# Second forward stage of a spectral block as runs of 32 half-width products, with rows and chunks requested a run ahead

## The chip, the cores and the metric

The kernel runs on one core of a Trainium2 chip. The metric is the device time of one execution in microseconds; the times given are medians of several executions. Engines are called PE (matmul), DVE (vector), ACT (scalar), POOL (GpSimd) and SP, whose queue issues all the DMA transfers of this kernel. A loaded weight tile and a matmul are two instructions of PE; the weight loads are listed as PEld.

## What is computed

For 8 sequences of 3136 positions and 256 channels: a real Fourier transform along the sequence, a complex 256 by 256 product with bias and soft threshold for each frequency, the inverse transform, and on its result y a mixing block: the real part of a two-dimensional transform is added, rows are normalised, and an MLP with 1024 hidden units is added to them.

```python
X = np.fft.rfft(x, axis=1);  Yr = Xr @ w_r - Xi @ w_i + b_r;  Yi = Xr @ w_i + Xi @ w_r + b_i
Y = soft_threshold(Yr, 0.01) + 1j * soft_threshold(Yi, 0.01)
y = np.fft.irfft(Y, n=3136, axis=1)
u = y + real(fft(fft(y, axis=1), axis=2))
un = (u - mean(u)) / sqrt(var(u) + 1e-6)
out = u + relu(un @ w_ch1) @ w_ch2
```

## The kernel before

The sequence length is split as 64 x 49. Work on each sequence b (0 to 7) is written as ten generators: p1 (first forward stage: products over the 64), p2_f2 (second forward stage: products over the 49, for both parts), p2_w (the complex product), p2_mix and p2_yt (mixing transform and transposes), p2_g2 (inverse over the 49), p3_norm (inverse over the 64, sum and normalisation), p3_tr (transposes), p3_mlp1 and p3_mlp2. Each generator yields a time of its own plan (in units of T, one sequence), and a heap resumes the one with the earliest time; so these times set the program order. A planner then puts the instructions of each engine in a fixed order by that priority and by what it expects to be ready. On the chip every engine works off its list in that order and waits where an operand or a buffer is not there.

Accumulators lie in eight PSUM banks: two for the MLP's first product (tile h, name h), two for its second (o), and four, tag g, that all other stages share (names g_f1, g_f2, g_w, g_mix, g_yt, g_g2, g_g1, g_ut). The MLP and most of the later stages use mm3: three products of rounded high and low parts (fp32r). The forward products of p1 and p2_f2 are plain f32; such a product becomes two weight loads and two matmuls on PE.

p2_f2 (lines 499 to 550) treats a sequence in four quarters q of eight frequencies. For each q, rows_f2 (line 484) requests two tiles af of 98 rows by 1024 and two tables tff (each of four frequencies, s = 0, 1). Then for four units ui it takes a bank and makes four products (line 523): weights are 128 columns of af (k = 0, 1), the moving operand is 100 columns of the table. ACT copies the bank to xx (line 539) and casts it to Xh (540); POOL or DVE subtracts (Xl); DVE adds the two parts (xs), ACT casts to Xsh (549), POOL subtracts to Xsl. For ui = 3 Xh is cast from the bank (545), one part is copied (546), and DVE does addition and Xl from the bank (547, 548). From sequence 2 on the work of a quarter is planned over 0.395 of its step, 0.25 T.

quarters (line 397) is used by p1 from sequence 1 on and by p3_norm. It makes eight products of 64 rows by 64 columns by 512 in four banks, for the four quarters of the array, as one block: small copies on ACT (line 403) hold the other banks until the rows have come, the first product waits for them, and the rest follow it directly.

ask (line 387) requests the chunks of x for p1 (tile xf, two buffers); from sequence 2 on it is called where the chunk's products are written. p3_norm requests bf (four buffers) and mt (two) for one pair of row groups at a time (load, line 799, called at line 820), just before its products at 832.

Of the kernel before, what the change touches and what calls it, by code (L numbers as in the profile page):

```python
# [20 lines left out]
D = 256  # L21
# [3 lines left out]
NM = 25  # L25
# [115 lines left out]
T1, ASK, BEHIND = (1.32, 0.25), 1.16, 3  # L141
WTIMES = (1.002, 1.003, 1.151, 1.152, 1.36, 1.42, 1.48, 1.54)
MLAG, NRM, TR = 1.874, -1.239, -0.86


@with_exitstack
def spectral_block(ctx: ExitStack, tc: tile.TileContext, x, w_ri, b_ri, w1, w2,
# [13 lines left out]
    def gtile(name):  # L161
        return ps.tile([128, 512], F32, tag="g", bufs=4, name=name)
# [146 lines left out]
    def after(*keys):  # L309
        while not all(k in done for k in keys):  # L310
            yield now[0] + 10
# [104 lines left out]
    def p1(b):  # L416

        if b == 0:
            yield from p1_first()
            return  # L420
        for i in (b, b + 1)[:1 + (b % 2 == 0)]:
            if i not in a_dram:
                ad = dr.tile([NM, 2, 2, U, D], F32, tag="ad", bufs=4, name=f"ad{i}")
                a_dram[i] = lambda u, ad=ad: (ad, u)
        todo = [(m, 4) for m in range(0, NM - 1, 4)] + [(NM - 1, 1)] * (b % 2 == 0)
        t0, width = T1 if b == 1 else (b - 0.3, 0.75) if b > 2 else (2.0, 0.48)
        rooms = [("W2", 1, 2), ("W3", 1, 2)] + [("utl", 2, 1)] * 2 if b == 1 else [("xf", 2, 1)] * len(todo)
        slots = [(tag, bufs, z, i) for tag, bufs, z in rooms for i in range(z)]
        evs = [("bf", 4)] * 4 + [("ev", 2)] * 2 if b == 1 else [("ev", 2)]
        pre = {}  # L430
        if b == 1:
            yield T * ASK
            for ci in range(len(todo)):
                ask(b, ci, todo, slots, pre)
        ci = 0
        while ci < len(todo):
            yield T * (t0 + width * ci / len(todo))
            if todo[ci][1] == 1:
                ask(b, ci, todo, slots, pre)
                m, xf = todo[ci][0], pre[ci]  # L440
                g = gtile("g_f1")
                te.matmul(g[:, :D], fwd_f, xf[:, :D], start=True, stop=True)
                ev = xf[:, D:2 * D]
                sc.copy(ev, g[:, :D])
                for r in range(2):
                    st_eng.dma_start(out=a_dram[b + r](0)[0][m, 0].rearrange("c u d -> (c u) d"), in_=ev[r * 64:r * 64 + 64])
                ci += 1
                continue
            groups = []
            for c in range(ci, ci + (1 if b == 1 else 2)):  # L450
                ask(b, c, todo, slots, pre)
                i = slots[c][3]
                xf = pre[c - i][:, i * 1024:i * 1024 + 1024]
                groups.append(([gtile("g_f1") for _ in range(2)],
                               [[xf[64 * r:64 * r + 64, p * 512:p * 512 + 512] for p in range(2)] for r in range(2)], xf[0:1, 0:2]))
            quarters(fwd_f, groups)
            for c, (banks, movs, late) in enumerate(groups, ci):
                xf, m = pre[c - slots[c][3]], todo[c][0]
                for r, g in enumerate(banks):
                    if b == 1:  # L460
                        tag, bufs = evs[(2 * c + r) % len(evs)]
                        ev = sb.tile([128, 512], F32, tag=tag, bufs=bufs, name="ev")
                    else:
                        ev = xf[:, r * 512:r * 512 + 512]
                    (va.tensor_copy if r and b != 1 else sc.copy)(ev, g)
                    st_eng.dma_start(out=n2_rows(a_dram[b](0)[0], m + 2 * r, 2), in_=ev.rearrange("p (n d) -> p n d", d=D))
            ci += len(groups)
        done.add(("a", b))

    def clock2(b, q):  # L470
        f2w, w0, ww = SHAPE if b else SHAPE0
        step = T * ((STEP0, STEP1)[b] if b < 2 else STEP)
        t0 = T * (1.0, START1)[b] if b < 2 else T * (b + 2 - LEAD - LAST * (b == NB - 1))
        return t0 + step * q, step, f2w, w0, ww, w0 + ww
# [3 lines left out]
    def x_tiles():  # L478


        return [sb.tile([128, 2] + c + [8, S], F32R, tag=t + z, bufs=1, name=t + z)
                for t, c in (("X", [2]), ("Xs", [])) for z in "hl"]

    def rows_f2(b, q, s):
# [11 lines left out]
            done.add(("af", 2 * q + s))  # L496
        return af, tff

    def p2_f2(b):


        for q in range(4):
            base, STEP, F2W, W0, WW, M0 = clock2(b, q)
            u0 = 8 * q
            yield base
            yield from after(("a", b, q) if b == 0 else ("a", b))
            if b == 0:
                X = sb.tile([128, 2, 2, 8, S], F32, tag=("Xh", "Xl")[q % 2], bufs=1, name="X")
                Xs = sb.tile([128, 2, 8, S], F32, tag=("Xsh", "Xsl")[q % 2], bufs=1, name="Xs")
                xt[b, q] = X, Xs  # L510
            else:
                xt[b, q] = Xh, Xl, Xsh, Xsl = x_tiles()
            afs, tfs = zip(*[rows_f2(b, q, s) for s in range(2)])
            for ui in range(4):
                yield base + STEP * ui * F2W / 4
# [251 lines left out]
    def p3_norm(b):  # L767

        def add(m, n, g, mt):

            ut = uts[b, m] = sb.tile([128, 2, D], F32, tag="ut", bufs=UTB, name="ut")
            va.tensor_add(ut[:, :n], g[:, :n * D].rearrange("p (n d) -> p n d", d=D), mt)  # L772
# [39 lines left out]
                af_ld.setdefault("mt", nc.sync.dma_start(out=mt[p:p + 32, :n], in_=mpn[:, n2:n2 + n]).ins)  # L812
            return mt, bfs
        pairs = ([[0], [4]] if b == 0 else [[0, 4]]) + [[8, 12], [16, 20]]
        for ms in pairs + [[NM - 1]] * (b % 2):
            n = 1 if ms[0] == NM - 1 else 4
            t0, T3 = clock3(b, ms[0])
            yield t0 + T3 * (NRM - 0.5 * (n == 1))
            yield from after(("b", b), ("m", b))
            loads = [load(m, n) for m in ms]  # L820
            if n == 1:
                mt, bfs = loads[0]
                g = gtile("g_g1")
                te.matmul(g[:, :D], inv_f, bfs[0][:, :D], start=True, stop=True)
                add(ms[0], 1, g, mt[:, :1])
                finish(ms[0], 1)
                continue
            if b == 0 and ms[0] == 0:
                yield from after(("w", 1, 0))
            groups = [([gtile("g_g1") for _ in range(2)], [[bfs[r][64 * p:64 * p + 64] for r in range(2)] for p in range(2)], bfs[0][0:1, 0:2])  # L830
                      for mt, bfs in loads]
            quarters(inv_f, groups, w_in[1, 0] if b == 0 and ms[0] == 0 else None)
            parts = [(m + 2 * p, g, mt[:, 2 * p:2 * p + 2]) for m, (mt, bfs), (banks, movs, late) in zip(ms, loads, groups) for p, g in enumerate(banks)]
            for m, g, mt in parts:
                add(m, 2, g, mt)
            for m, g, mt in parts:
                finish(m, 2)

# [165 lines left out]
```

## Time and profile before

| | us |
|---|---|
| median of 3 runs (1840.67 to 1847.36) | 1842.6 |
| profiled execution | 1843.72 |
| its span, first to last instruction | 1841.9 |
| PE busy | 1803.2 |
| DVE, ACT, POOL busy | 1210.2, 808.3, 564.8 |

Times in the rows are microseconds from the start of the span unless marked ns. Busy time is the time in which at least one instruction of an engine ran. Matmuls are pipelined: a record lasts from its start until its last result is written, and the next one starts before that. The chain that ended last is followed back from the last instruction, at each step to what released it. A line such as L175 can be that of a helper (mm3), so the tile names tell the stage.

### The profile page before, as it was taken

What the parts mean: (1) busy time and instruction counts of PE and PEld (TensorE: products, weight loads), DVE (VectorE), ACT (ScalarE), POOL (GpSimd) and SP (SyncE); (2) the same over time, 40 slices, a digit from 0 to 9 for tenths busy, and PEclk for the clock granted to TensorE, in tenths of its full rate; (3) what the DMA queues carried; (4) which work ended last, traced back from release to release, by engine and by line L of the source; (5) the groups of instructions that cost most, each with busy time, mean ns of one, the idle gap of its engine ahead of it and who ended that gap; (6) DMA issues with size and microseconds to landing.
All of it is one profiled execution on the core that took longest, in us unless ns stands there. A gap on an engine that the chain in (4) does not pass through costs nothing.

```text
span 1841.9 us, 29443 instructions
## 1 busy us (share of the span) xinstructions
PE 1803.2 (98%) x10082; PEld 1500.9 (81%) x10082; DVE 1210.2 (66%) x2619; ACT 808.3 (44%) x1914; POOL 564.8 (31%) x1021
## 2 busy tenths in 40 slices
PE   8988899999999999999999999999999999999998
PEld 5667688888888988888888988888888898878888
DVE  3866767676577766765776766757657767755543
ACT  2564454544445534444544444444444454322222
POOL 0003434333234332342432333423324334221110
PEclk8999899999999999999999999999999999999999
DMA  8766553554436533374515734345533533152211
GB/s 255 233 208 168 147 189 100 161 153 145 130 82 198 163 120 106 100 206 125 175 46 141 217 122 134 99 132 163 152 99 90 177 90 104 57 151 67 60 35 34
DMA packets 157936, 245.61 MB, mean 133 GB/s; under 512 B 24209, under 2 KB 105177, under 8 KB 157529
## 3 DMA queue, kind: packets, MB, share of 16 engines
q1 hardware_dynamic: 157784, 243.72, 45.2%
q8 instruction: 80, 1.31, 0.3%
q14 instruction: 72, 0.58, 0.1%
HBM read 140.79 MB, written 102.86 MB: 132 GB/s over the span
## 4 chain that ended last, share of the span: by engine, by line
PE 87%; DVE 5%; DMA 3%; SPq 2%; ACT 1%; issue 1%; POOL 1%; DVEq 0%; ACTq 0%; POOLq 0%
PE o L175 28%; PE h L175 27%; PE g_w L175 9%; PE g_f L523 5%; PE g_g L175 4%; PE g_yt L723 3%; PE g_g L402 2%; PE g_ut L853 2%; PE g_f L402 2%; PE g_w L569 2%; PE g_mix L660 1%; PE g_mix L662 1%; DMA out_dram<-total 1%; DMA md<-mq 1%; DVE ut L772 1%
## 5 line engine op out<-in xcount | busy, mean ns | idle before, releaser
L872 DVE SCALAR_TENSOR_TENSOR hl<-h,hh 128x512 fp32r<-128x512 f32 (+2 forms) x416 | 271.6, 655 | 391.2 <-ACT hh L871 388.2
L871 ACT ACTIVATE hh<-h 128x512 fp32r<-128x512 f32 (+2 forms) x416 | 237.5, 572 | 503.8 <-PE h L175 463.1
L175 PE MATMUL o<-hl,w2h 128*128 128x512 f32 (+2 forms) x832 | 329.0, 396 | 2.8 <-DVE hl L872 2.6
L175 PE MATMUL h<-utl,w1h 128*128 128x512 f32 (+2 forms) x832 | 319.5, 384 | 3.9 <-DVE hl L872 3.9
L175 PE MATMUL o<-hh,w2l 128*128 128x512 f32 (+2 forms) x832 | 318.5, 383 | 0.0
L175 PE MATMUL o<-hh,w2h 128*128 128x512 f32 (+2 forms) x832 | 317.1, 381 | 0.0
L175 PE MATMUL h<-uth,w1l 128*128 128x512 f32 (+2 forms) x832 | 316.0, 380 | 0.0
L175 PE MATMUL h<-uth,w1h 128*128 128x512 f32 (+2 forms) x832 | 315.7, 379 | 0.0
L879 POOL TENSOR_TENSOR total<-uth,utl 128x256 f32<-128x256 f32 x200 | 149.4, 772 | 476.4 <-DMA out_dram<-total 263.5
L175 PEld LDWEIGHTS o<-hl,w2h 128*128 128x128 f32 x832 | 157.0, 189 | 47.6 <-DVE hl L872 20.7
L175 PEld LDWEIGHTS h<-utl,w1h 128*128 128x128 f32 x832 | 156.7, 188 | 34.9 <-DVE hl L872 6.9
L175 PEld LDWEIGHTS h<-uth,w1l 128*128 128x128 f32 x832 | 156.8, 188 | 29.3 <-issue 1.6
L175 PEld LDWEIGHTS h<-uth,w1h 128*128 128x128 f32 x832 | 156.9, 189 | 27.8 <-issue 2.4
L175 PEld LDWEIGHTS o<-hh,w2l 128*128 128x128 f32 x832 | 156.7, 188 | 27.3
L175 PEld LDWEIGHTS o<-hh,w2h 128*128 128x128 f32 x832 | 157.2, 189 | 19.2
L523 PEld LDWEIGHTS g_f<-tff,af 98*128 98x128 f32 x1024 | 135.5, 197 | 14.2 <-issue 4.6
L523 PE MATMUL g_f<-tff,af 98*128 98x100 f32 x1024 | 141.5, 279 | 5.4 <-DMA aq<-ev 3.4
L586 POOL TENSOR_TENSOR Y<-y,m 128x400 f32<-128x400 f32 x56 | 66.9, 1195 | 191.0 <-DVE m L585 182.4
L583 DVE SCALAR_TENSOR_TENSOR y<-g_w,small,ks 128x400 f32<-128x400 f32 x128 | 80.3, 628 | 51.7 <-PE g_w L175 38.6
L168 POOL TENSOR_TENSOR Xl<-xx,Xh 128x400 fp32r<-128x400 f32 x81 | 89.8, 1110 | 57.2 <-ACT Xh L540 43.8
L754 ACT COPY bev<-g_g 98x512 f32<-98x512 f32 x128 | 74.7, 584 | 42.9 <-PE g_g L175 30.0
L165 DVE TENSOR_TENSOR yl<-g_yt,yh 100x512 fp32r<-100x512 f32 x112 | 76.3, 684 | 15.1 <-ACT yh L732 13.3
(163 smaller groups left out, 3286.3 us busy)
## 6 DMA issues: line engine op xcount, KB each, us to landing
bd<-bev SPq DMA_DIRECT2D x128, 196.0 KB
mt<-md SPq DMA_DIRECT2D x192, 128.0 KB
bf<-bd SPq DMA_DIRECT2D x96, 256.0 KB
out_dram<-total SPq DMA_DIRECT2D x88, 256.0 KB
af<-ad SPq DMA_DIRECT2D x56, 392.0 KB
md<-mq SPq DMA_DIRECT2D x112, 192.0 KB
xf<-in_x SPq DMA_DIRECT2D x39, 512.0 KB
ad<-xf SPq DMA_DIRECT2D x72, 256.0 KB
```

The source lines that it names most:

```text
L165: va.tensor_sub(out_, full, hi.bitcast(F32))
L168: gp.tensor_sub(out_, full, hi.bitcast(F32))
L175: last = te.matmul(o, l, r, start=start and i == 0, stop=stop and i == 2)
L402: return te.matmul(banks[i][64 * j:64 * j + 64], mat[rows, rows], movs[i][j], start=True, stop=True)
L523: te.matmul(gf[:, k, :, s], afs[s][:, ui * D + k * 128:ui * D + k * 128 + 128], tfs[s][:, ui].rearrange("p (c j) -> p c j", c=2), start=Tr ...
L583: va.scalar_tensor_tensor(y1, gw, bias[:, c, o:o + 1], ks, op0=ALU.add, op1=ALU.add)
L586: (va if b == 0 or o == 0 else gp).tensor_sub(y[:, o, :, c, :], y1, m)
L723: te.transpose(gt[:100, (v * 2 + o) * 128:(v * 2 + o + 1) * 128], y[:, o, place].rearrange("p c j -> p (c j)"), ident)
L754: sc.copy(bev, g[:98])
L871: sc.activation(hh[:, :w], h[:, :w], AF.Relu)
L872: va.scalar_tensor_tensor(hl[:, :w], h[:, :w], 0.0, hh[:, :w].bitcast(F32), op0=ALU.max, op1=ALU.subtract)
L879: gp.tensor_add(total[:, k, cols], uth[:, k, cols].bitcast(F32), utl[:, k, cols].bitcast(F32))
```

## The change

From sequence 2 on, the second forward stage is a new generator, burst. For each quarter it takes all four g banks at once, has ACT hold three of them with small copies that wait for the other row tiles, and makes the 32 products of the quarter without a break: each former product of 128 columns becomes two of 64 columns, whose results lie in the lower and the upper 64 partitions of the bank. Then ACT copies the four banks to four tiles xx (two of them in the room of tag ev), the rows of the next quarter are requested, and the further steps follow at the times they had, 0.03 of a step later; the fourth unit takes them from xx as the others do, and its two subtractions run on DVE. The rows of a sequence's first quarter are requested 0.3 of a step ahead.

For p1 from sequence 2 on, the first two chunks are requested 0.08 T ahead and each next two as soon as the two before them are written. In p3_norm of every sequence the first pair's rows are requested 0.3 of a group's step ahead, and the next pair's rows after the sums of the pair before.

```diff
+EARLY, BURST = 0.3, 0.03
@@ p1
         ci = 0
+        if b > 1:
+            yield T * (t0 - 0.08)
+            for c in range(2):
+                ask(b, c, todo, slots, pre)
         while ci < len(todo):
...
             ci += len(groups)
+            if b > 1:
+                for c in range(ci, min(ci + 2, len(todo))):
+                    ask(b, c, todo, slots, pre)
@@ new generator
+    def burst(b, q, rows):
+        base, STEP, F2W, W0, WW, M0 = clock2(b, q)
+        Xh, Xl, Xsh, Xsl = xt[b, q]
+        afs, tfs = zip(*rows)
+        yield base + STEP * BURST
+        banks = [gtile("g_f2") for _ in range(4)]
+        lates = (afs[1][0:1, 0:2], tfs[1][0:1, 0, 0:2], tfs[0][0:1, 0, 0:2])
+        held = [sc.copy(g[0:1, 0:2], late) for g, late in zip(banks[1:], lates)]
+
+        def prod(ui, s, k, h):
+            gf = banks[ui][64 * h:64 * h + 64, :400].rearrange("p (k c s j) -> p k c s j", k=2, c=2, s=2)
+            first = ui * D + k * 128 + h * 64
+            return te.matmul(gf[:, k, :, s], afs[s][:, first:first + 64], tfs[s][:, ui].rearrange("p (c j) -> p c j", c=2), start=True, stop=True)
+        todo = [(ui, s, k, h) for ui in range(4) for s in range(2) for k in range(2) for h in range(2)]
+        first = prod(*todo[0])
+        for h in held:
+            tc.add_manual_dep(first.ins, h.ins.name, ...)
+        with tc.high_priority(), tc.issue_after(first.ins):
+            for args in todo[1:]:
+                prod(*args)
+        xxs = []
+        for ui, g in enumerate(banks):
+            xx = sb.tile([128, 2, 2, 2 * S], F32, tag=("xx", "ev")[ui // 2], bufs=2, name="xx")
+            sc.copy(xx, g[:, :400].rearrange("p (k c t) -> p k c t", k=2, c=2))
+            xxs.append(xx)
+        rows[:] = [rows_f2(b, q + 1, s) for s in range(2)] if q < 3 else []
+        for ui, xx in enumerate(xxs):
+            yield base + STEP * (BURST + ui * F2W / 4)
+            us = slice(2 * ui, 2 * ui + 2)
...
+            lo_x = lo_v if ui == 3 else lo_g
+            xs = sb.tile([128, 2, 2 * S], F32, tag="xs", bufs=2, name="xs")
+            sc.copy(xh, xx)
+            lo_x(xl, xx, xh)
+            va.tensor_add(xs, xx[:, :, 0], xx[:, :, 1])
+            sc.copy(xsh, xs)
+            lo_x(xsl, xs, xsh)
@@ p2_f2
+        nxt = []
+        if b > 1:
+            base, STEP, F2W, W0, WW, M0 = clock2(b, 0)
+            yield base - STEP * EARLY
+            yield from after(("a", b))
+            nxt += [rows_f2(b, 0, s) for s in range(2)]
...
+            if b > 1:
+                yield from burst(b, q, nxt)
+                continue
@@ p3_norm
-        for ms in pairs + [[NM - 1]] * (b % 2):
+        pairs += [[NM - 1]] * (b % 2)
+        t0, T3 = clock3(b, 0)
+        yield t0 + T3 * (NRM - EARLY)
+        yield from after(("b", b), ("m", b))
+        ready = [load(m, 4) for m in pairs[0]]
+        for ms, then in zip(pairs, pairs[1:] + [[]]):
             n = 1 if ms[0] == NM - 1 else 4
             t0, T3 = clock3(b, ms[0])
             yield t0 + T3 * (NRM - 0.5 * (n == 1))
-            yield from after(("b", b), ("m", b))
-            loads = [load(m, n) for m in ms]
+            loads = ready
...
+            def ask_next():
+                return [load(m, 1 if m == NM - 1 else 4) for m in then]
...
             for m, g, mt in parts:
                 add(m, 2, g, mt)
+            ready = ask_next()
             for m, g, mt in parts:
                 finish(m, 2)
```

## Rows read from the trace of the kernel before

**Rows 1.** The page: busy time of each engine; chain that ended last, by line.

```profile
PE 1803.2 (98%) x10082; PEld 1500.9 (81%) x10082; DVE 1210.2 (66%) x2619; ACT 808.3 (44%) x1914; POOL 564.8 (31%) x1021
...
PE o L175 28%; PE h L175 27%; PE g_w L175 9%; PE g_f L523 5%; PE g_g L175 4%; PE g_yt L723 3%; PE g_g L402 2%; PE g_ut L853 2%; PE g_f L402 2%; PE g_w L569 2%; PE g_mix L660 1%; PE g_mix L662 1%; DMA out_dram<-total 1%; DMA md<-mq 1%; DVE ut L772 1%
```

**Rows 2.** By stretch: length; busy PE, PEld, DVE, ACT, POOL; granted clock; DMA share, GB/s.

```profile
290.00:1580.00 1290.00, 1286.97 (x7456) 1095.31 (x7455) 885.35 (x1920) 595.36 (x1424) 462.28 (x797) 1.00 0.45 132
```

**Rows 3.** Last of three waits of PE, 290 to 1580: us in total, times, longest.

```profile
PE o L175 <- DVE hl L872: 0.3, 1, 0.3
```

**Rows 4.** Instructions on tile af, 290 to 1580: min/median/max ns, first and last start.

```profile
L523 PE MATMUL g_f<-tff,af x768: 249/275/353, 300.2 to 1560.4; 98*128 98x100 f32 x192
```

**Rows 5.** Timeline of PE, two stretches: start, length, line, output<-operands, shapes, count.

```profile
473.67 0.39 PE L175 MATMUL h<-uth,w1h 128*128 128x512 f32 x1
473.90 0.39 PE L175 MATMUL h<-uth,w1l 128*128 128x512 f32 x1
474.13 0.58 PE L523 MATMUL g_f<-tff,af 98*128 98x100 f32 x4
...
474.81 0.40 PE L175 MATMUL o<-hh,w2h 128*128 128x512 f32 x1
...
470.48 1.03 PE L523 MATMUL g_f<-tff,af 98*128 98x100 f32 x8
471.29 0.34 PE L175 MATMUL g_g<-yl,tih 100*98 100x256 f32 x1
```

**Rows 6.** One run of line 402: timeline of PE and PEld, then counts in 50 ns.

```profile
565.01 0.39 PE L175 MATMUL h<-uth,w1l 128*128 128x512 f32 x1
565.33 1.95 PE L402 MATMUL g_f<-xf,fwd_f 64*64 64x512 f32 x16
...
567.54 0.40 PE L175 MATMUL o<-hh,w2h 128*128 128x512 f32 x1
...
565.81 0.15 PEld L402 LDWEIGHTS g_f<-xf,fwd_f 64*64 64x64 f32 x4 [0.28 <-issue]
566.24 0.15 PEld L402 LDWEIGHTS g_f<-xf,fwd_f 64*64 64x64 f32 x4 [0.28 <-issue]
...
565.30:565.35 0.05, 0.03 (x4) 0.03 (x4) 1.00 0.34 123
```

**Rows 7.** Line 402 from 290 to 1580: min/median/max ns, first and last start.

```profile
L402 PE MATMUL g_g<-bf,inv_f x288: 589/589/641, 293.7 to 1537.3; 64*64 64x512 f32 x144
L402 PEld LDWEIGHTS g_f<-xf,fwd_f x240: 129/133/133, 348.7 to 1337.5; 64*64 64x64 f32 x120
L402 PE MATMUL g_f<-xf,fwd_f x240: 589/589/640, 348.7 to 1337.9; 64*64 64x512 f32 x120
```

**Rows 8.** Transposes of 128 columns: timeline of PE; durations from 470 to 480.

```profile
475.42 0.60 PE L723 MATMUL g_yt<-ident,Y 128*100 128x128 f32 x4
...
L723 PE MATMUL g_yt<-ident,Y x8: 271/272/273, 469.8 to 475.7; 128*100 128x128 f32 x8
```

**Rows 9.** Timeline of PE ahead of these transposes.

```profile
475.36 0.22 PE L662 MATMUL g_mix<-cs,el 128*100 128x128 f32 x1
```

**Rows 10.** Timeline of PE behind the run of line 402 at 400.8.

```profile
403.08 0.50 PE L175 MATMUL o<-hl,w2h 128*128 128x512 f32 x1 [0.35 <-DVE hl L872]
```

**Rows 11.** Groups from 290 to 1580: busy us, mean ns | idle before, its ends.

```profile
L539 ACT COPY xx<-g_f 128x400 f32<-128x400 f32 x72 | 35.5, 493 | 11.5 <-PE g_f L523 10.3 <-POOL vv L794 0.7 <-POOL Xl L168 0.6
...
L403 ACT COPY g_f<-xf 1x2 f32<-1x2 f32 x45 | 6.6, 150 | 16.9 <-DVE ut L772 7.6 <-DVE y L583 4.9 <-DVE utl L165 3.5
...
L165 DVE TENSOR_TENSOR el<-eo,eh 128x400 fp32r<-128x400 f32 x48 | 38.4, 801 | 3.1 <-ACT eh L630 3.1
```

**Rows 12.** Waits of PE: one of the whole span, one from 1580 to 1842.

```profile
PE g_g L402 <- DMA bf<-bd: 2.2, 1, 2.2
...
PE g_ut L853 <- DVE ut L772: 2.7, 2, 2.5
```

**Rows 13.** Waits of SP's queue from 290 to 1580: us in total, times, longest.

```profile
SPq L806 <- PE g_g L402: 71.4, 18, 17.2
```

More of the change, by code (lines that the diff above doesn't have):

```diff
@@ L497, in rows_f2 @@
         return af, tff
-    def p2_f2(b):
+    def burst(b, q, rows):
[13 more added lines that the diff above has]
+        for h in held:
+            tc.add_manual_dep(first.ins, h.ins.name, mybir.DependencyInfo(mybir.DependencyClass.Sync, mybir.DependencyReason.DATA), reason="bank held")
+        with tc.high_priority(), tc.issue_after(first.ins):
[10 more added lines that the diff above has]
+            us = slice(2 * ui, 2 * ui + 2)
+            xh, xl = (t[..., us, :].rearrange("p k c s j -> p k c (s j)") for t in (Xh, Xl))
+            xsh, xsl = (t[..., us, :].rearrange("p k s j -> p k (s j)") for t in (Xsh, Xsl))
+            lo_x = lo_v if ui == 3 else lo_g
[5 more added lines that the diff above has]
+            lo_x(xsl, xs, xsh)
@@ L505, in p2_f2 @@
             yield base
-            yield from after(("a", b, q) if b == 0 else ("a", b))
+            if b < 2:
+                yield from after(("a", b, q) if b == 0 else ("a", b))
             if b == 0:
```

## The prediction, made before the change was run

> **What bounds the kernel now.** I read the page's busy times and its chain first [rows 1]: PE is busy for 98% of the span, and the chain that ended last runs through its products, those of the MLP (tiles o and h) alone being 55% of it. A busy PE need not be a PE at its peak, so the table by stretch comes next [rows 2]: between 290 and 1580 us PE idles for 3 of 1290 us at the full clock (1.00, the upper of its two levels, 2.4 GHz), while DVE is busy for 69%, ACT for 46% and POOL for 36% of that stretch. The list of PE's waits there has three rows, none of them at the second stage; the last is shown [rows 3]. All second-stage products of sequences 2 to 7 (768 matmuls, four runs for each of six sequences, so 24 runs of 32) lie between 300 and 1560 us [rows 4]. In that stretch PE works off a fixed list without gaps: what a product costs is the distance from its start to the next one's, and the span changes by the difference of those distances. Waits of other engines and of transfers count only where they reach PE.
>
> **The products now.** An f32 product is two matmuls, each with a weight load. The timeline has an h product at 473.90, four second-stage matmuls, one o product and a second one at 474.81 [rows 5]. Undisturbed MLP matmuls stand 0.23 apart; from 473.90 to 474.81 is 0.91, less twice 0.23 leaves 0.45 for four, 0.1125 each. Eight behind short transposes: 471.29 - 470.48 = 0.81, or 0.101. Most runs are of the first kind; I take 0.111: 32 x 0.111 = 3.55 us a run, 24 x 3.55 = 85.2 us in all.
>
> **The products after.** A run becomes 32 products, so 64 matmuls, on two halves of 64 columns, with all 98 rows in both. No row of this trace has that shape. The nearest is the 64x64 run of line 402, where products on different quarters of the array lie side by side: four matmuls start within 50 ns at 565.30, and 16 matmuls of 0.59 each are done in 1.95 [rows 6, 7]; four weight loads take 0.15 together, where one takes 0.13 [rows 6, 7]. The quarters include two column halves on the same rows, which is what the change uses. So I take the two halves as fully side by side: 32 steps, not 64.
>
> A step's length: a wave of 512 columns lasts 0.43 (weight loads at 565.81 and 566.24 [rows 6]); four transposes of 128 columns last 0.60 with the last one 0.272 long [rows 8], so (0.60 - 0.272) / 3 = 0.109. Along the line through both, 100 columns take 0.109 - 28 x (0.43 - 0.109) / 384 = 0.086. Today's step is longer, 0.1125, because 128 columns of weights are loaded for each 100 streamed; a load of 64 columns shows as 51 ns where nothing hides it (the first wave's matmuls last 640 instead of 589 ns [rows 7]), so the load no longer sets the step.
>
> Entering and leaving the split array costs too: from 565.01 to 567.54 is 2.53; less 2 x 0.23 and four waves of 0.43, 0.36 is left [rows 6]. Today's runs pay none of that. A run after: 32 x 0.086 + 0.36 = 3.11 us. **The sum on PE:** 3.55 - 3.11 = 0.44 a run, 24 x 0.44 = 10.6 us less. Bounds of the step: 0.085 if matmuls alone set it, 0.1125 if the pair goes no faster than one product now (32 x 0.1125 + 0.36 = 3.96, 24 x 0.41 = 10 us more). I take 0.086, since in line 402 four loads side by side were as quick as one.
>
> **What the runs ask of the others.** All four g banks must be free at once. Line 402 does this 33 times in the stretch already (288 and 240 matmuls, 16 a run [rows 7]); PE's one wait of 0.35 us right behind such a run stands at 403.08 [rows 10], and the list, whose only wait at an o product this is, has none at their entry [rows 3]. 24 x 0.35 / 33 = 0.3 us, so I book nothing between 0 and 1 us. A bank is complete after 16 matmuls, 8 steps or 0.69 us, and its evacuation takes 0.49 [rows 11], so three of four banks are free when the run ends. If instead each run cost that 0.35, it would be 8 us.
>
> ACT gets three small copies (0.15 each), and for the fourth unit it copies to xx and casts from there, where it cast and copied half from the bank: at most one more evacuation of 0.49 [rows 11]. That is 0.94 a run, 23 us in all, on an engine that is idle for 54% of the stretch. The small copies wait on ACT for rows and banks; behind them in its queue stand the relu casts hh, on which DVE's hl and then PE's o products hang; the 0.35 above is such a wait. DVE takes Xsl's subtraction of the fourth unit over from POOL, 200 columns, half of el's 0.80 [rows 11], and reads xx instead of the bank in two more, for which I book as much again: 0.8 a run, 20 us of its 405 idle ones. POOL loses the 24 subtractions. All of it lies beside PE; if it did not, its bound is the 0.35 a run above.
>
> **The earlier requests.** Nothing is fetched more often: per run two af and two tff transfers, per pair of chunks two xf, per norm pair four bf and eight mt, all on SP's queue, in another order. A request waits at the head of that queue until its buffer is free, and stores of bd, md and the output stand behind it. SP already waits 71 us in 18 pieces for bf's buffers, up to 17.2 [rows 13], and PE shows none of that in the stretch. The gain is bounded by PE's waits, in the whole span, that end with such transfers: 2.2 for bf, and 2.7 at g_ut behind the sum ut, which reads mt [rows 12], so at most 5 us. The bound below is a late set of rows: the queue's longest block of 17.2 is shorter than a run's distance (some 54 us, 290 to 1580 over 24), so a request that much ahead covers it; 0 to 3 us lost. I take nothing on either side, because the requests in the trace already stand at the queue's head when their buffer comes free [rows 13].
>
> **Total.** The profiled execution took 1843.7 (span 1841.9 and 1.8 around it), 1.1 above the median of 1842.6. 1843.7 - 10.6 = 1833.1, or 1832.0 against the median: **1832 us**, 0.6% faster. A measurement of this kernel can tell about 0.5% (9.2 us) from no change; the line is at 1833.4.
>
> **The rivals.**
> 1. *Banks give it back.* 33 runs of line 402 and 24 new ones now each empty the g banks; if each new run costs the 0.35 us of [rows 10], 8 us return: 1840. For it: 57 instead of 33 such points in the stretch, and MLP work alone must fill them. Against it: only one of 33 shows it. 0.25.
> 2. *The stream of instructions becomes the bound* (slower). In the run PE needs a matmul with its own weights each 0.043 us; the nearest row is a spacing of 0.06 (475.36 to 475.42 [rows 8, 9]), and that not sustained. At 0.06 a run takes 64 x 0.06 + 0.36 = 4.20, 0.65 more, 24 x 0.65 = 15.6: 1858. It decides from 0.050 (even: 64 x 0.05 + 0.36 = 3.56) and passes the line of 0.5% at 0.056. Against it: the four starts within 50 ns [rows 6]. 0.08.
> 3. *Loads wait for the other half.* If a half's weight load could not run while the other half's matmul does, a step would be 0.086 + 0.051 = 0.137, a run 4.74, 24 x 1.19 = 29 us more: 1871. Against it: in line 402 loads go out at 565.81 and 566.24, in the middle of the 1.95 us of matmuls, with all four quarters of the array at work [rows 6]. The Trainium skill (TensorE: Matmul & The Clock Gate, Part 3, what overlaps and what doesn't) says that a weight load overlaps matmuls in flight only where the row groups differ; both new halves use the same rows, so by that rule this rival would hold, and the trace's loads of line 402 speak against it, though those quarters also have two row halves. 0.04.
> 4. *The change does not do what it says*: the halves go one after the other. 64 x 0.086 + 0.36 = 5.86, 24 x 2.31 = 55 us more: 1898. Against it [rows 6] as above. 0.03.
> 5. *More than the sum*: the waits for bf and mt go too, up to 5 us: 1827. 0.08.
>
> **How the numbers follow.** The forecast holds with 0.52, its own range 1829 to 1836, from 0 to 1 us of waits and 3 us either way for the requests. Above 1846 lie rivals 2 to 4 (0.15), below 1826 some 0.03 of the fifth; so the range is 1826 to 1846, which takes the 1840 in. Faster by over 0.5% (below 1833.4): 0.36 of the forecast's 0.52 and the fifth's 0.08, 0.44. Slower by over 0.5%: most of rivals 2 to 4, 0.13. Within: 0.43.
>
> **What would show it.** In the trace after: second-stage matmuls of 64 columns, 1536 in the stretch, 24 blocks of 64 without a gap; a block 32 x 0.086 + 0.275 (the last one's own length) = 3.0 us long, and 3.1 from the start of the product before it to the second one behind, less 2 x 0.23. A block near 4.2 would be rival 2, 4.7 the third, 5.9 the fourth. PE's waits in the stretch stay near 3 us; some 8 us more, behind hl or at the entry of the blocks, would be the first. ACT up by some 20 us, DVE by 20, POOL down. The prediction is wrong if blocks are 3.0 us long and the span still falls by under 5 us, or if the requests move stores so far back that waits appear in the first 290 us.

## The result, and the profile after

The changed kernel takes 1858.0 us (median, 1854.87 to 1859.94) against 1844.6 for the kernel before on the same chip: ratio 1.0072, interval 1.0050 to 1.0093. It is slower, where 1832 was forecast. 1858 is also the number of the second rival; that is chance, as the rows show. The profiled execution took 1854.9, its span is 1853.1.

The page of the kernel after, busy times and chain by line (they answer to [rows 1]):

```profile
PE 1798.5 (97%) x10850; PEld 1480.2 (80%) x10850; DVE 1243.8 (67%) x2643; ACT 822.1 (44%) x1986; POOL 557.8 (30%) x997
...
PE o L176 26%; PE h L176 26%; PE g_w L176 9%; PE g_g L176 4%; PE g_f L520 3%; PE g_yt L781 2%; PE g_ut L919 2%; PE g_f L403 2%; PE g_g L403 2%; PE g_mix L718 1%; DVE eo L682 1%; DMA mt<-md 1%; PE g_w L627 1%; DVE hl L938 1%; DVE ut L830 1%
```

The span is 11 us longer and PE is busy for 5 us less: the second stage has fallen from 5 to 3% of the chain, and lines of DVE have come into it. The products themselves, by line and in the timeline of PE (answering [rows 4, 5]; the first two lines are min/median/max ns):

```profile
L520 PEld LDWEIGHTS g_f<-tff,af x1536: 132/137/137, 305.8 to 1568.5; 98*64 98x64 f32 x192
L520 PE MATMUL g_f<-tff,af x1536: 249/249/301, 305.8 to 1568.6; 98*64 98x100 f32 x192
...
305.49 0.39 PE L176 MATMUL o<-hh,w2l 128*128 128x512 f32 x1
305.81 2.97 PE L520 MATMUL g_f<-tff,af 98*64 98x100 f32 x64
308.71 0.36 PE L718 MATMUL g_mix<-cs,eh 128*100 128x256 f32 x1
```

All 64 matmuls of a run are one block of 2.97 us; from its first start to the next product's it is 2.90. Over the 24 runs, with what they stretch the products ahead of and behind them against undisturbed ones, the second stage costs about 73 us where it cost about 86: 12 to 13 less, a little more than the forecast's 10.6. So the time was lost elsewhere. The table by stretch and the list of PE's waits for 290 to 1580 (answering [rows 2, 3]) say where; ahead of them stand the two rows of the list of before that [rows 3] leaves out:

```profile
PE g_w L175 <- POOL Xsl L168: 1.8, 2, 1.1
PE g_g L175 <- DVE yl L165: 0.7, 1, 0.7
...
290.00:1580.00 1290.00, 1272.59 (x8157) 1064.90 (x8156) 912.81 (x1931) 604.69 (x1489) 455.42 (x773) 1.00 0.45 132
...
PE o L176 <- DVE hl L938: 7.7, 11, 1.8
PE g_g L176 <- DVE yl L166: 3.4, 1, 3.4
PE o L176 <- DVE rb L969: 3.4, 4, 1.1
PE g_mix L718 <- DVE ut L830: 0.8, 1, 0.8
```

With five smaller rows PE now waits 17.0 us in this stretch, in place of 2.8. None of these waits stands at a block's entry; most stand at o products of the MLP, behind DVE.

I set the n-th product h<-uth,w1h of both traces side by side, as a ruler that the change does not touch. The 33rd starts at 250.9 before and 251.9 after; the 673rd at 1608.2 and 1621.8. So the 11.2 us by which the span grew are 1.0 ahead of them, 12.7 between them, and 2.5 that come back behind them, where the wait of 2.5 for ut in [rows 12] had a clock drop behind it and the wait of 1.9 in its place has none. The longest wait stands at the first run of sequence 2. The 65th product, at 328 before, is 9.3 late there, 8.3 more than the 33rd. Not all of that is lost: the new order has put other work ahead of this product (g_g, g_w and g_mix products, some 3 us net), and at the 101st the lag is down to 2.1 again. The wait and the halved clock behind it, some 5.3 us more than before, are the loss at this place. What happens there, in the timelines of PE and of DVE, and in the table by stretch:

```profile
313.08 0.64 PE L781 MATMUL g_yt<-ident,Y 128*100 128x128 f32 x4 [0.23 <-ACT xx L531]
317.12 0.53 PE L176 MATMUL g_g<-yl,tih 100*98 100x256 f32 x1 [3.41 <-DVE yl L166]
...
310.00 1.56 DVE L682 SCALAR_TENSOR_TENSOR eo<-Y,mask 128x200 f32<-128x200 f32 x2 [1.77 <-POOL Y L644]
311.48 0.35 DVE L543 TENSOR_TENSOR xs<-xx 128x200 f32<-128x200 f32 x1
312.35 1.18 DVE L543 TENSOR_TENSOR xs<-xx 128x200 f32<-128x200 f32 x1 [0.52 <-POOL Xsl L169]
...
316.39 0.68 DVE L166 TENSOR_TENSOR yl<-g_yt,yh 100x512 fp32r<-100x512 f32 x1
...
316.00:318.00 2.00, 0.88 (x4) 0.88 (x5) 2.00 (x6) 1.74 (x6) 2.00 (x3) 0.50 0.11 23
318.00:320.00 2.00, 2.00 (x10) 1.90 (x9) 2.00 (x4) 0.96 (x2) 2.00 (x2) 0.50 0.00 0
320.00:322.00 2.00, 2.00 (x6) 1.52 (x6) 2.00 (x3) 0.62 (x1) 1.57 (x3) 0.50 0.31 100
```

PE's list has the inverse product g_g directly behind the transposes g_yt whose result it needs by way of yl. Its other operand, yh, is there at 314.62 on ACT, behind the run's last xx; yl runs at 316.39 on DVE, behind ten operations there since 310.00, two of them the run's xs. PE stands still for 3.41 us, and from 315.6, still in that wait, to 322.4 the granted clock is at its lower level (0.50 is 1.2 GHz); PE works for 5.3 of these 6.8 us, MLP products 0.43 apart instead of 0.23, so about 2.6 us are lost once more. In the trace of before 7.0 us of work and a wait of 0.70 stand between the same two products, from 311.47 to 319.19: eight second-stage matmuls and 24 of the MLP.

```profile
319.19 0.37 PE L175 MATMUL g_g<-yl,tih 100*98 100x256 f32 x1 [0.70 <-DVE yl L165]
```

### The profile page after: what moved, and what is told of

Read it like the earlier page. It is cut to its first block, busy times and chain, and to the rows that moved or that the text cites. A ratio compares the mean times of both kernels' runs of the same rounds, so it can differ in the third digit from the quotient of the medians.

```text
span 1853.1 us, 31040 instructions
## 1 busy us (share of the span) xinstructions
PE 1798.5 (97%) x10850; PEld 1480.2 (80%) x10850; DVE 1243.8 (67%) x2643; ACT 822.1 (44%) x1986; POOL 557.8 (30%) x997
## 4 chain that ended last, share of the span: by engine, by line
PE 80%; DVE 9%; DMA 5%; SPq 1%; issue 1%; ACT 1%; POOL 1%; DVEq 0%; POOLq 0%; ACTq 0%
PE o L176 26%; PE h L176 26%; PE g_w L176 9%; PE g_g L176 4%; PE g_f L520 3%; PE g_yt L781 2%; PE g_ut L919 2%; PE g_f L403 2%; PE g_g L403 2%; PE g_mix L718 1%; DVE eo L682 1%; DMA mt<-md 1%; PE g_w L627 1%; DVE hl L938 1%; DVE ut L830 1%
## 5 line engine op out<-in xcount | busy, mean ns | idle before, releaser
L176 PE MATMUL o<-hl,w2h 128*128 128x512 f32 (+2 forms) x832 | 330.1, 397 | 13.8 <-DVE hl L938 9.8
L543 DVE TENSOR_TENSOR xs<-xx 128x200 f32<-128x200 f32 x96 | 77.6, 810 | 24.2 <-POOL Xsl L169 11.8
L781 PE MATMUL g_yt<-ident,Y 128*100 128x128 f32 x512 | 82.5, 278 | 3.0 <-DVE y L641 1.1
```

Of the source, the lines that this page charges most:

```text
L176: last = te.matmul(o, l, r, start=start and i == 0, stop=stop and i == 2)
L543: va.tensor_add(xs, xx[:, :, 0], xx[:, :, 1])
L781: te.transpose(gt[:100, (v * 2 + o) * 128:(v * 2 + o + 1) * 128], y[:, o, place].rearrange("p c j -> p (c j)"), ident)
```

## The experiments

Times are medians; ratios are to the kernel before on the same chip, with their intervals. "At 0.03" is the place of a run in its step, BURST in the diff. "Runs alone" is the change without its earlier requests; full products, two banks and the last two lines are the whole change, requests included.

| kernel | us | ratio |
|---|---|---|
| the change | 1858.0 | 1.0072 (1.0050 to 1.0093) |
| requests alone | 1847.2 | 1.0019 (1.0007 to 1.0030) |
| runs alone, 0.03 | 1853.2 | 1.0052 (1.0035 to 1.0069) |
| full products: runs of 16 | 1863.2 | 1.0106 (1.0089 to 1.0122) |
| two banks: two runs of 16 half products | 1863.7 | 1.0105 (1.0090 to 1.0120) |
| runs alone, sums and low parts on POOL | 1855.3 | 1.0059 (1.0037 to 1.0080) |
| evacuation alone | 1846.8 | 1.0013 (0.9999 to 1.0027) |
| runs alone, from sequence 3 | 1849.3 | 1.0029 (1.0017 to 1.0040) |
| runs alone, 0.06 | 1845.3 | 1.0010 (1.0000 to 1.0020) |
| runs alone, 0.12 | 1840.7 | 0.9983 (0.9973 to 0.9992) |
| runs alone, 0.20 | 1842.3 | 0.9989 (0.9978 to 1.0000) |
| the change, 0.12 | 1843.3 | 1.0004 (0.9993 to 1.0014) |
| the change, 0.12, low parts on POOL | 1847.2 | 1.0024 (1.0011 to 1.0037) |

### One part at a time

**Requests alone:** the products of before, with all earlier requests.

```diff
+            rows = nxt if b > 1 else [rows_f2(b, q, s) for s in range(2)]
+            afs, tfs = zip(*rows)
...
+                if b > 1 and ui == 3:
+                    nxt = [rows_f2(b, q + 1, s) for s in range(2)] if q < 3 else []
```

> The kernel before with the earlier requests alone (chunks of p1, rows of the second stage a run ahead, rows of p3_norm); products of 128 columns as before. In the trace after, the 24 blocks cost PE 12.4 us less than the products they replace, and all other products together cost 23.6 us more. Block theory (a block of four banks makes PE and DVE wait around it): no block, so no change, 1841 to 1848. Request theory (the earlier requests reorder SP's queue and buffers, and PE pays for it): the 23.6 us come without the gain, 1868. Order theory (any edit of the program order moves the planner's list, waits fall anywhere): within 10 us of before on either side, with waits at other places.

3 us slower. By the ruler its trace is 2.7 us behind that of before at 154 us and at 1608, and never differs from that by more than 0.1 in between; PE's three waits of [rows 3] stand unchanged. With the old products the requests give nothing and cost nothing in the steady stretch. The 3 us lie ahead of 154 us, where of the requests only those of p3_norm fall (in all six traces with the requests the ruler's first product starts later than before, by 0.3 to 6.3 us; in the seven without them sooner, by 0.3 to 3.6); the wait of 2.2 for bf in [rows 12], which they should have ended sooner, is there as before (in the whole change it is 4.2):

```profile
PE g_g L403 <- DMA bf<-bd: 2.0, 1, 2.0
```

**Runs alone:** the change without the earlier requests; a run asks for its rows where the kernel before did.

```diff
-                yield from burst(b, q, nxt)
+                yield from burst(b, q, [rows_f2(b, q, s) for s in range(2)])
```

> The changed kernel with the requests as in the kernel before; the blocks of 32 half-width products stay. Block theory: as the changed kernel, 1854 to 1862, PE's waits at o products behind DVE hl as there (about 8 us from 290 to 1580 against 0.3 before). Request theory: blocks gain their 12 us undisturbed, 1832. Order theory: between these, and the waits at other places than in the changed kernel.

9 us slower: the run is what costs most. PE waits 14.6 us in the stretch; the 3.4 for yl, the clock drop behind it and the 1.2 at 350.5 of the whole change are there. Its two longest waits at o products, 1.8 us each at 604 and 1487, are not. In the whole change these two come from further off, here in the timelines of POOL, DVE and PE:

```profile
600.83 2.25 POOL L945 TENSOR_TENSOR total<-uth,utl 128x256 f32<-128x256 f32 x4 [11.63 <-DMA out_dram<-total]
603.39 0.18 DVE L844 BATCH_NORM_AGGREGATE ag<-st 128x2 f32<-128x6 f32 x1 [2.99 <-POOL vv L847]
603.99 0.39 PE L176 MATMUL o<-hl,w2h 128*128 128x256 f32 x1 [1.78 <-DVE hl L938]
```

POOL's total waits until a store of the output has landed; the step vv stands behind it on POOL, ag behind vv on DVE, hl behind ag, and the o product needs hl. At 1487 it is the same row. In the trace of before POOL waits for DVE there, not for a store. In the runs alone the store at the first place goes out 1.2 us sooner (592.15 against 593.32), POOL's total starts 3.1 us sooner, and PE does not wait. By the ruler the runs alone lose 9.5 us between the 33rd and the 673rd product and the whole change 12.7: together with the runs, the requests do cost some 3 us in the stretch. Which request makes the store late was not tested.

**Full products:** the whole change, but 16 products of 128 columns per quarter in one block, so the array is not split.

```diff
-            first = ui * D + k * 128 + h * 64
+            first = ui * D + k * 128
...
-        todo = [(ui, s, k, h) for ui in range(4) for s in range(2) for k in range(2) for h in range(2)]
+        todo = [(ui, s, k, h) for ui in range(4) for s in range(2) for k in range(2) for h in range(1)]
```

> The changed kernel with 16 products of 128 columns in a block in place of 32 of 64; four banks, holds and requests stay. A block then costs 32 x 0.1125 = 3.60 instead of 3.05. Block theory and request theory: the changed kernel's waits stay and 24 x 0.55 = 13 us come on top, 1871. A third theory, that the split array itself slows its neighbours: without it the 23.6 us are gone, 1845.

Slower still, with waits of 12.8 us in sum. The top of PE's list, 290 to 1580:

```profile
PE o L176 <- DVE hl L938: 7.5, 10, 4.6
PE o L176 <- DVE rb L969: 3.4, 4, 1.1
```

Nine of these waits stand at the same products as in the change, with the same length to 0.03 us. The 3.4 for yl is gone; in its place the first run of sequence 2 has one of 4.6 at an o product, behind hl, with the clock at 0.50 for 6.8 us around its end. So it is not the split array that makes the waits. Against this kernel, which has all of the change but the halves, the halves save 5 us (1863.2 to 1858.0): the 12 to 13 us that the products gain, less what the waits, 4.2 us longer in the change, and other places give back.

**Two banks:** the whole change with two blocks of 16 half products a quarter, each in two banks.

```diff
+        for pair in range(2):
+            yield base + STEP * (BURST + pair * F2W / 2)
+            banks = [gtile("g_f2") for _ in range(2)]
...
+            todo = [(ui, s, k, h) for ui in (2 * pair, 2 * pair + 1) for s in range(2) for k in range(2) for h in range(2)]
```

> The changed kernel with the block cut in two: 16 half-width products in two banks, then 16 in two banks a fifth of a step later. PE: two blocks of 16 x 0.086 + 0.29 = 1.67, 3.33 a quarter against 3.55 before, 24 x 0.22 = 5 us less. Block theory: two banks stay with the other stages, so about half of the 23.6 us is left: 1844 - 5 + 12 = 1851. Request theory: 1844 - 5 + 24 = 1863. Split-array theory: twice as many entries, the 23.6 double: 1886.

```profile
PE o L176 <- DVE hl L940: 9.7, 5, 4.8
PE g_f L517 <- DVE yl L166: 2.4, 3, 1.5
```

Missed: half the banks and half the block do not halve the loss. The wait for yl at the first run is down to 1.5 us (+1.7 us by the ruler at 328), but two others at hl, of 4.8 and 3.4 us, come at 604 and 1050, each with the clock at 0.50 for 6.8 us around its end. Both have the row behind them that the whole change has at 604: POOL's total stands for 15.1 and 12.4 us until a store of the output has landed, and DVE's ag for 5.8 and 3.4 behind it. How many banks are held at once is not what decides; the order in the lists of the engines and of SP's queue is.

### Whose queue

**Less for DVE:** runs alone, with the sums xs and the fourth unit's low parts on POOL.

```diff
-            lo_x = lo_v if ui == 3 else lo_g
+            lo_x = lo_g
...
-            va.tensor_add(xs, xx[:, :, 0], xx[:, :, 1])
+            gp.tensor_add(xs, xx[:, :, 0], xx[:, :, 1])
```

> The runs of 64 half products without the earlier requests (1853.2 us alone), and of the pile that each run leaves on VectorE the four sums xs and the two low parts of the fourth unit go to GpSimd. Theory A, VectorE's queue: o products wait because hl stands on VectorE behind that pile. Then the rows 'PE waits for hl' (4.4 us in 10 waits) and the wait of 3.4 us for yl at 317 fall to under 2 us in sum, the gain of about 12 us on PE shows, and the time is 1832 to 1837. Theory B, the hold: PE's list has nothing left to do while four banks are taken at once, whoever empties them; the waits stay and the time is 1850 to 1856. If GpSimd becomes the late one instead, waits for its rows appear at g_g and the time is above 1856.

```profile
290.00:1580.00 1290.00, 1273.51 (x8156) 1066.01 (x8155) 814.96 (x1785) 604.45 (x1486) 533.96 (x914) 1.00 0.45 132
...
PE o L176 <- DVE hl L916: 4.2, 8, 1.7
PE g_g L176 <- DVE yl L166: 4.1, 1, 4.1
PE o L176 <- DVE rb L947: 3.4, 4, 1.1
```

DVE is busy for 98 us less than in the change, and PE's waits are 16.3 us in sum where the runs alone have 14.6. That DVE has too much to do, my theory then, does not explain them. It is no test of less work alone, though: POOL, 78 us busier, got the work.

**Evacuation alone:** the kernel before, with its fourth unit worked from xx and its low parts on DVE.

```diff
-                if ui < 3:
+                if ui < 3 or b > 1:
+                    if b > 1 and ui == 3:
+                        lo_x = lo_v
```

> The kernel before, with only the evacuation changed: the fourth unit of each second-stage run from sequence 2 on is copied to xx by ScalarE and worked from there, its low parts on VectorE; its products stay in four groups with other work between. Theory A, VectorE's load as such: 24 x 0.8 us more on it bring waits of PE for hl, 1846 to 1852. Theory B, it is the bunching of the four units and not the load: no new wait, 1843 to 1845 against 1844.

```profile
PE h L175 <- DVE hl L874: 3.4, 2, 2.1
PE o L175 <- DVE hl L874: 1.4, 3, 0.5
PE g_g L175 <- DVE yl L165: 0.7, 1, 0.7
```

Between the theories: by the ruler 4.1 us more in the steady stretch, in five waits for hl (one of them there before), while the interval of the times reaches to no change. So by this trace the evacuation is a part, and the smaller one.

### Where the run stands

**From sequence 3:** runs alone, with `b > 2` in place of `b > 1` ahead of burst.

> The runs without the earlier requests, from sequence 3 on only (20 runs instead of 24). Theory A, the place: the wait of 3.4 us at 317 and the 6.8 us of halved clock behind it belong to the first run of sequence 2, where the last work of the sequence before stands on VectorE; without it the loss of some 8 us there is gone and 4 x 0.5 us of gain with it: 1845 to 1847 against 1853.2. Theory B, whichever run comes first pays that: the same wait and fall of the clock stand at the first run of sequence 3, 1852 to 1855.

The first run now is that of sequence 3, and it pays nothing: the longest wait for yl is 0.7, as before, and no clock drop comes there. 1849.3 lies between the two expectations. By the ruler the trace agrees with before to 0.1 us from 415 to 507, where the runs alone had lost 5.3 net in sequence 2, but from there on it loses 7.0, nearly 3 more than the runs alone do. So those 5 us belong to sequence 2, the wait and the clock at its first run above all; some 7 us come elsewhere.

**Later places:** runs alone, at 0.12, then at 0.06 and 0.20 of the step.

```diff
-EARLY, BURST = 0.3, 0.03
+EARLY, BURST = 0.3, 0.12
```

> The runs without the earlier requests, each put at 0.12 of its step instead of 0.03 (some 5 us later in the planned order). Theory A, the block itself makes the waits: they stay at some 11 us in sum at other places, and the time is 1850 to 1857. Theory B, an unlucky order: where the block falls among the MLP's work decides, and the time moves by over 5 us, down to 1840 if the run of sequence 2 no longer meets the pile of the sequence before.

> The runs of 64 half products without the earlier requests, each at 0.06 of its step (0.03 gave 1853.2, 0.12 gave 1840.7). Theory A, the order: the block frees some 13 us of PE's time wherever it stands, its fewer neighbours cost some 9 us of waits in any place (MLP products that stood with second-stage groups between them now follow each other), and one bad spot, the first run, costs 8 us more at 0.03. 0.06 lies nearer to the bad place: 1842 to 1853, the wait at about 317 there or not. Theory B, the waits grow with the distance from the place that the list was tuned for (0.03 to 0.32): then 0.06 lies between 1849 and 1853.

> The same at 0.20 of the step. Theory A, the order: no wait of over 2.5 us, so no halved clock in the steady stretch, and waits of some 8 to 12 us in sum: 1838 to 1846. If lateness of the X tiles decides instead (g_w products wait for Xh and Xl, since they are due at 0.569 of the step): new waits at g_w, 1846 to 1860.

The place decides: 1853.2, 1845.3, 1840.7 and 1842.3 us, with nothing else changed. At 0.12 the kernel is 0.17% faster than before, the best of all. At 0.06 the g_g product of the first run has ten MLP products ahead of it, and waits 0.58 us where it waited 3.41 at 0.03; no clock drop follows. Its timeline of PE:

```profile
311.20 0.60 PE L767 MATMUL g_yt<-ident,Y 128*100 128x128 f32 x4
...
313.70 0.39 PE L176 MATMUL h<-uth,w1l 128*128 128x512 f32 x1
314.66 0.36 PE L176 MATMUL g_g<-yl,tih 100*98 100x256 f32 x1 [0.58 <-DVE yl L166]
```

By the ruler the kernel at 0.03 is 7.5 us behind that at 0.06 by the 101st product, with the wait at 317, its clock drop and the wait at 350 behind it; 2 us of that come back later. But the other loss stays at each place. PE's waits at 0.12, 290 to 1580:

```profile
PE g_yt L767 <- POOL Y L630: 3.2, 3, 1.7
PE h L176 <- DVE hl L916: 2.5, 3, 1.5
PE o L176 <- DVE hl L916: 1.6, 4, 0.5
PE o L176 <- DVE rb L947: 1.5, 3, 0.6
PE g_g L403 <- ACT bev L798: 1.3, 2, 0.6
```

These sum to 10.1; at 0.06 it is 11.9, at 0.20 10.8, before 2.8. From the 33rd to the 673rd product of the ruler the four places take 1366.7, 1361.2, 1356.3 and 1357.3, before 1357.2: at the best place the products' 12 us are paid back almost to the last one. What 0.12 is faster by comes in good part ahead of 251 us, where the text of both kernels is the same (3.3 us there in the profiled execution); so I claim of it no more than its interval says.

**The whole change at 0.12**, and the same with the fourth unit's low parts on POOL (`lo_x = lo_g`):

> The whole change, requests too, with the runs at 0.12 of the step instead of 0.03. If place and requests are independent: 1840.7 and the 3 us that the requests cost before 154 us, 1842 to 1845. If the requests change the order around the runs as well: below 1840 or above 1848.

> As the run of the whole change at 0.12, with the two low parts of the fourth unit on GpSimd like those of the other three, so 48 operations leave VectorE. Theory A, VectorE's load is a part of the waits (the evacuation alone cost 4 us): 2 to 5 us less than the run at 0.12 with them on VectorE. Theory B, the place in PE's list alone makes them: no difference beyond 1 us.

1843.3, as forecast for independent parts: 2.6 us for the requests, where alone they cost 3.0. At 0.03 they are less independent: there the requests add 4.9 to the runs (1853.2 to 1858.0), and the place gives 14.8 with them (1858.0 less 1843.3) and 12.5 without. The second was a miss for both theories: with 20 us less on DVE (919.5 to 899.0 in the stretch) and 33 more on POOL, the waits for hl at o products rise from 1.6 to 5.3, and 4 us are lost.

## Why the prediction was wrong

**The products: right, some 2 us short.** Blocks are 2.97 us long where 3.0 was forecast. Step 0.086: so the starts stand (526.675, 526.761 in the first steps of one block). Entering and leaving, booked at 0.36 from [rows 6], came to 0.29 (0.09 ahead of the block, 0.05 in its first step, 0.15 behind). The old products were worth about 86, as taken. With that the second, third and fourth rival are refuted: their blocks would have been 4.2, 4.7 and 5.9 us long. The Trainium skill's rule (TensorE: Matmul & The Clock Gate, Part 3, what overlaps and what doesn't) that a weight load overlaps matmuls in flight only where the row groups differ does not describe this block: 64 loads of 0.132 and 64 matmuls of 0.249, all on the same rows, lie within 2.97 us.

**The step that failed: "I book nothing between 0 and 1 us" and "All of it lies beside PE".** Waits of PE in the stretch rose by 14.2 us, and the halved clock behind one of them cost some 2.6 more. Two things were wrong in it. First, I asked whether the others were idle on average, and priced the entry into a block by the runs of line 402. The entry is free, as booked: none of the longer waits stands there. And I misread the one wait that I priced. The 0.35 at 403.08 [rows 10] is not one behind ACT's small copies, as the prediction has it: in the trace of before hh ends at 398.94, and hl starts 3.41 us later because two operations eo stand ahead of it on DVE, for the first of which DVE waits 0.95 us on POOL. Late operands behind such rows are what came, at more places. Second, the sum on PE took its order as given ("PE works off a fixed list without gaps"): the list is fixed on the chip, but the change gives another list, for every engine and for SP's queue. The next place behind the one at 317 shows it at an o product, first before, then after, in the timelines of PE and of DVE:

```profile
344.32 0.39 PE L175 MATMUL o<-hl,w2h 128*128 128x512 f32 x1
...
337.46 0.69 DVE L872 SCALAR_TENSOR_TENSOR hl<-h,hh 128x512 fp32r<-128x512 f32 x1 [2.14 <-ACT hh L871]
...
348.90 0.39 PE L176 MATMUL o<-hh,w2l 128*128 128x512 f32 x1
350.49 0.50 PE L176 MATMUL o<-hl,w2h 128*128 128x512 f32 x1 [1.20 <-DVE hl L938]
...
346.91 1.78 DVE L682 SCALAR_TENSOR_TENSOR eo<-Y,mask 128x200 f32<-128x200 f32 x2
348.61 0.62 DVE L641 SCALAR_TENSOR_TENSOR y<-g_w,small,ks 128x400 f32<-128x400 f32 x1
349.16 0.67 DVE L972 TENSOR_TENSOR total<-total,rb 128x512 f32<-128x512 f32 x1
349.76 0.68 DVE L938 SCALAR_TENSOR_TENSOR hl<-h,hh 128x512 fp32r<-128x512 f32 x1
```

Before, the same o product (the 67th) stood 7.9 us behind the start of its last h product, and hl ran 0.03 us after hh; after, it stands 4.8 behind, and hl runs 3.0 after hh, at the end of a row of DVE's other work.

That the old products had been cover, short work between an h product and the o product that needs its hl, would be the obvious reading, and the traces bear it out only in small part. The change has eleven waits for hl at o products, 7.7 us in sum, where before had the one of [rows 10]. In the trace of before, second-stage products stand between the same h and o products at five of them (1.9 us in sum), and at the other six (5.8 us), the one above among them, there is none. What grew at these is the time from hh to hl, other than at 410, where the wait of [rows 10] stands as before: from 0.03 to 3.0 us at 350.5, from 1.0 to 4.2 at 604, from 0.9 to 4.0 at 1487, from 0.1 to 3.4 at 852 and 1291. At 317 eight of the 32 matmuls that stood between g_yt and g_g were second-stage ones; the other 24, of the MLP, were moved by the planner.

**The first rival** named the right kind of wait (behind hl) with half the size and the wrong source, the banks: two banks in place of four give longer waits, not shorter ones.

**ACT and DVE.** ACT rose by 13.8 over the span (23 was the upper end). DVE rose by 33.6 where 20 were booked, though its new work is what was counted: xs from xx went from a median of 366 ns to 914, as the last section shows. That nothing of it reaches PE was wrong too: of the evacuation alone some 4 us do, by the one trace of it.

**The requests: 0 was right for the stretch with the old products, 3 us too good for the start, and some 3 too good for the stretch with the runs.** The prediction had named stores that stand behind requests and booked nothing for them; the waits at 604 and 1487 end a chain that starts at such a store. No gain of the up to 5 us came, so the fifth rival fell too.

**The chances.** 0.13 for slower were those of the second to the fourth rival, all about PE's blocks, and none of them happened. What happened had no place in the list: a loss by the order of the list itself. A change that takes small products out from between others at over a hundred places should have had that as its rival on the slow side. The trace of before shows how near it was: at six of the eleven places where an o product later waits for hl, hl was done less than 0.4 us ahead of its product.

**What stays open.** Of the 25 us by which all but the second-stage products became longer in the steady stretch, 14.2 are listed waits, 2.6 the clock, and some 5 to 6 the products on both sides of a wait (an estimate from 0.16 us ahead of the wait of 1.20 at 350.5 and 0.10 behind it, for 20 waits more than before); 2 to 3 I can put at no place. Why the planner's new order is worse, and which part of the change moves it, is not settled: work moved from DVE to POOL did not lower the waits at 0.03 and raised them at 0.12, and each place of the run has others. That 0.12 is a better place than 0.03 is shown; that it is so because the first run's g_g has other products ahead of it is shown for that run alone, at 0.06. Half-width products left in the groups of before were not run, so the halves are priced in a block alone. Which operation costs the requests' 3 us at the start was not found.

## What to carry to other kernels

Ahead of drawing scattered small work on a full engine into one block, list the operands that in the trace of before come just in time: the gain on the engine came whole here, and six of the eleven waits for hl stand at such places. Follow a wait back to its start, since the engine that it names may itself stand behind another one or behind a store. Where an order is planned from due times, one edit moves every list: try the new work at several due times before judging it (here 12.5 us between two places, as much as the edit gains). Where the n-th products of two traces are set side by side, count the other work ahead of them too, or moved work looks like lost time. Part the change early: here requests, width, block and place could each be priced by a kernel of its own.

## What the runs showed of the hardware

**Two column halves on the same rows** run side by side: 64 f32 matmuls of 98 rows by 64 columns by 100 in 2.97 us, a pair each 0.086 us.

**A long wait cost more than its length:** PE's 3.41 us of standing still at 317 brought 6.8 us at half the clock, 5.3 of them in its work. The same came in four other kernels, at waits of 3.4 to 4.8 us; at 0.06, where the wait is 0.58, it did not. Between these lie two stretches of 3.4 us at 0.50: at 1478 with the sums on POOL, around a wait of 1.9, and at 1472 in the runs from sequence 3, around two waits of 1.0 and 1.1 us. Waits of 1.8 us at 604 and 1487 in the change had none.

**DVE and POOL get in each other's way on tiles that both read from SBUF.** The sums xs of the kernels before and after, min/median/max ns:

```profile
L542 DVE TENSOR_TENSOR xs<-xx x72: 325/366/2231, 305.3 to 1559.4; 128x200 f32<-128x200 f32 x72
L547 DVE TENSOR_TENSOR xs<-g_f,im x24: 332/366/368, 319.7 to 1563.0; 128x200 f32<-128x200 f32 x24
...
L543 DVE TENSOR_TENSOR xs<-xx x96: 329/914/1362, 307.9 to 1571.5; 128x200 f32<-128x200 f32 x96
```

Read from a bank of PSUM (second line) the sum never takes over 0.37 us, though POOL runs at the start of 7 of the 24. Read from xx, in the trace after, 75 of 96 start while an operation of POOL runs, and these take 0.93 on average; the other 21 take 0.36. POOL beside the two xs shown above, at 311.48 (0.35) and 312.35 (1.18):

```profile
311.57 0.75 POOL L169 TENSOR_TENSOR Xsl<-xs,Xsh 128x200 fp32r<-128x200 f32 x1
312.27 1.04 POOL L169 TENSOR_TENSOR Xl<-xx,Xh 128x400 fp32r<-128x400 f32 x1
```

The second one starts behind POOL's Xl and ends 0.2 us after it, as 71 of the 75 do (0.22 to 0.29 us after the operation of POOL in which they start). The first, ahead of Xsl and with only a short step of POOL before it, is quick. The Trainium skill (SBUF — State Buffer, SBUF: two separate sides) says the same: an operation of DVE with two SBUF inputs and one of POOL take a shared pair of ports as a lock, whole instructions long. So moving a sum's operand from a bank to SBUF, as the change does for the fourth unit, has a price that the sum's duration alone does not show.
